# Rows gathered up to three units ahead and scaled in pieces, second products two columns behind the first

## The chip, the core and the metric

The kernel runs on one core of a Trainium2 chip. The core has five engines with an instruction queue each: TensorE (PE; its weight loads are listed as PEld), VectorE (DVE), ScalarE (ACT), GpSimd (POOL) and SyncE (SP), which here only issues transfers. Every queue is worked off in order. The metric is device time in microseconds (us), from first to last instruction of one launch. The kernel before took 943.5 us as the median of three timed runs (942.85 to 946.33). A change of 0.5% or less (4.7 us) counts as no change.

## The reference, cut to what matters

```python
def _attn_ref(q, k, v, tau):              # 8 batches, 8 heads, 576 tokens, 64 wide
    scores = (1 / sqrt(64)) * q @ k.T
    thresh = max(scores, -1) - tau
    scores = where(scores >= thresh, scores, -1e9)
    attn = exp(scores - max(scores)); attn /= sum(attn) + 1e-9
    return attn @ v

def _moe_ref(x, w_gate, w_output_gate, w1, w2):   # x: 4608 rows of 512; 8 experts, 1024 hidden
    logits = x @ w_gate; e_idx = argmax(logits); gate_w = softmax(logits)[e_idx]
    eom = sigmoid(x @ w_output_gate)
    for e in range(8):
        mask = e_idx == e
        h = maximum(x[mask] @ w1[e], 0); ye = h @ w2[e]
        out[mask] = gate_w[mask] * eom[mask, e] * ye
```

## The kernel before, in words

**Attention** (class Attention) runs first, in 144 steps, nine for a pair of units; a unit is one head of two batches. TensorE forms scores and their transposes, VectorE negates them and takes the minimum (L159) and masks the exponentials (L189), ScalarE takes the exponentials. Finished rows of 512 features, with gate weight and token number behind them, are routed and written by GpSimd's scatters to a table in device memory, `xs` (L547). Scatters of the first three batch pairs are called "A", those of the last pair "B". After B, eight "pad" scatters (L720) write empty rows behind each expert's last row.

**The experts** (class Experts) run as 13 units of one expert each, on rows that a gather on SP's queue brings from `xs` into a tile `xg`. Units 0, 1 and 2 are fixed groups of 366, 256 and 424 rows of experts 0 to 2, made of A rows alone. Units 3 to 12 have 420, 256, 512, 256, 504, 256, 396, 256, 256 and 496 rows; a table that VectorE fills step by step (`choose`) says which expert and rows they are. In what follows a unit of 256 rows is narrow, the others are wide. Each unit has eight **columns** of 128 hidden features. In column f TensorE does the first products of f (`first`, L1216, into `ph`), ScalarE applies the ReLU and rounds the result to 16 bits (`hr`, `hh`), VectorE forms the rest (`hl`, L955), and TensorE does the second products (`second`, L1238 to L1241; L1337 to L1340 in the "Turned" units 2, 3 and 9), which need `hh` and `hl`. Before, the second products of a column come right after the first products of the next.

Weights come in chunks of two columns. Each chunk is loaded, measured (largest value: VectorE's maximum L859 and ScalarE's `junk`, L867), scaled by a power of two and split into 16-bit high parts (ScalarE, L951) and low parts (VectorE, `w1l`, `w2l`, L957). The rows are treated alike: `even` finds the largest value of each row (`ax`, L911) and scales the tile (L916), four scalings for a wide unit; `prep` transposes it (TensorE, `px`, L1192 or L1314) and splits it (`xh`, `xl`). All this for unit i+1 is done during unit i: `even` at one go in column 3, `prep` in columns 5 and 6. Turned units are turned back by `flip` (L1354), which with `prep`, `top` and `spread` (two small products on the weights' scale) shares two tiles `px`.

The program order of TensorE, VectorE, ScalarE and GpSimd is the order in which the code is written (`manual_schedule`); `run` (L1064) writes it column by column. Transfers have their waits from the tiles and the rows of `xs` that they touch. Before, the scatters of A, B and pad are one group of the table to the framework, so a gather waits also for scatters whose rows it does not read.

Of the kernel before, what the change touches and what calls it, by code (L numbers as in the profile page):

```python
# [17 lines left out]
P = 128  # L18
# [412 lines left out]
class Router:  # L431
# [4 lines left out]
    def __init__(self, ctx, tc, ntok, E, DM, sizes, cut):  # L436
# [58 lines left out]
        self.gate, self.kind, self.pads = None, None, []  # L495
# [50 lines left out]
    def scatter(self, src, idx, group):  # L546
# [10 lines left out]
        return ins  # L557

    def route(self, bp, rows, LX):
# [82 lines left out]
        for b in range(n):  # L642
            yield "scatter"
            self.tok.append(("A" if split else "B", self.scatter(rows[:, b, :], dsti[:, b : b + 1], "tok")))
# [132 lines left out]
class Experts:  # L777
    RB, NW, YB = 4, 4, 4
    UNITS = (0, 6, 2, 7, 3, 8, 1, 5, 9, 4)
    TURN = (2,)  # L780
    LOOK, MEASURE = 3, 3

    def __init__(self, ctx, tc, rt, ident, w1, w2, out):
# [3 lines left out]
        self.raw = [self.pool("eraw", self.RB)]  # L787
        self.mp = self.pool("em", 1)
        self.junk = self.mp.tile([P, 1024], BF16, name="junk")
        self.early = self.mp.tile([P, 2 * rt.early, 4], F32, name="early")  # L790
        self.part = self.mp.tile([P, 1], F32, name="part")
# [3 lines left out]
        self.gp = self.pool("eg", 1)  # L795
# [9 lines left out]
    def open(self):  # L805
        self.px = lambda: [self.ps_x.tile([P, 512], F32, name="px") for _ in range(2)]
        self.hp = self.pool("eh", 2)
        self.ph = lambda: self.ps_h.tile([P, 512], F32, name="ph")
        self.hidden = lambda n: [self.hp.tile([P, 512], dt, name=x) for x, dt in (("hr", F32), ("hh", F16), ("hl", F16))]
        self.xp = self.pool("ex", 2)  # L810
        self.fp = self.pool("ef", 1)
        self.raw.append(self.pool("eraw1", self.RB))
        self.ahead = self.RB
        self.load_next()
        self.wp += [self.pool(f"ew{i}", 1) for i in range(1, self.NW)]
        for name, bufs in (("y", 4), ("h", 2), ("x", 2)):
            setattr(self, f"ps_{name}", self.pool(f"ps_{name}", bufs, space=PSUM))

# [36 lines left out]
    def measure(self, raw, mx, g, half=None):  # L855
        nc = self.nc
        flat = lambda r: r.rearrange("p c f -> p (c f)")
        if half is None:
            nc.vector.tensor_reduce(mx[:, 0, g : g + 1], flat(raw[0]), axis=AX.X, op=ALU.max, apply_absolute_value=True)  # L859
        else:  # L860
            part = flat(raw[0])[:, half * 512 : half * 512 + 512]
            to = mx[:, 0, g : g + 1] if half == 0 else self.part
            nc.vector.tensor_reduce(to, part, axis=AX.X, op=ALU.max, apply_absolute_value=True)
            if half == 0:
                nc.vector.tensor_tensor(to, to, self.part, op=ALU.max)
        if half != 1:
            nc.scalar.activation(self.junk, flat(raw[1]), AF.Abs, accum_out=mx[:, 1, g : g + 1])  # L867
# [40 lines left out]
    def even(self, xg):  # L908
        nc, n, DM = self.nc, xg.shape[1], self.rt.DM
        ax, up, down = (self.kp.tile([P, 4], F32, name=x)[:, 0:n] for x in ("ax", "xup", "xdown"))  # L910
        nc.vector.tensor_reduce(ax, xg[:, :, 0:DM], axis=AX.X, op=ALU.max, apply_absolute_value=True)  # L911
        nc.vector.tensor_scalar(ax, ax, UP, FLOOR, op0=ALU.mult, op1=ALU.max)
        self.powers(up, down, ax)
        for t in range(n):
            x = xg[:, t, 0:DM]
            nc.vector.tensor_scalar(x, x, up[:, t : t + 1], None, op0=ALU.mult)  # L916
        return down
# [51 lines left out]
    def begin(self):  # L969
# [7 lines left out]
        self.halves, self.ready, self.ahead, self.due = [], [], 0, None  # L977
        self.first_raws, self.column, self.fresh, self.mx, self.diag = [], 0, [], {}, None
        self.order = [(e, g) for e in (*range(1, rt.early), 0) for g in range(4)]
# [5 lines left out]
    def size(self, j, half=None):  # L985
        e, g = self.order[j]
        raw = self.first_raws[j]
        self.measure(raw, self.early[:, 2 * e : 2 * e + 2], g, half)
        if e == 0 and half != 1:
# [3 lines left out]
    def settled(self, i):  # L993
# [566 lines left out]
```

## Time and profile before

The profiled execution took 940.68 us with a span of 939.0 us; the median of the timed runs is 943.5 us.

| engine | busy us | share of the span | instructions |
|---|---|---|---|
| PE | 882.4 | 94% | 8367 |
| PEld | 539.5 | 57% | 8367 |
| DVE | 794.7 | 85% | 1940 |
| ACT | 708.8 | 75% | 1367 |
| POOL | 388.0 | 41% | 660 |

Busy time counts an instruction from its start to its end; matmuls overlap, so that a busy TensorE can still be waiting for less than the length of a matmul. Attention takes about the first half of the span; the first second products of unit 0 begin at 478.43 us. In the rows below, "[13.50 <-DVE hl L955]" means that the engine was idle for 13.50 us before this instruction, and that the instruction of line 955 which writes `hl` released it.

### The profile page before, as it was taken

Reading aid. Unit: us, or ns where it says so; the run is one execution under the profiler, and the core shown is the slowest. Engines: PE = TensorE matmul, PEld = TensorE weight load, DVE = VectorE, ACT = ScalarE, POOL = GpSimd, SP = SyncE. Lnnn points to the kernel's source line nnn. Section 1 sums busy time; section 2 is a strip of 40 time slices with the busy share of each in tenths; the row PEclk is TensorE's granted clock in tenths of the full one; section 3 lists DMA queues with packets and bytes.
Section 4 is the critical chain, followed back from the end, with each engine's and each line's share of the span. In section 5 each row is a group of like instructions: output and inputs, shape, how many; then the busy total and the mean of one; then the engine's idle time right before and its main releaser. Section 6 shows DMA issues by size and latency. Waiting matters only on the chain. (4 is left out here: it accounts for less than half of the span.)

```text
span 939.0 us, 22600 instructions
## 1 busy us (share of the span) xinstructions
PE 882.4 (94%) x8367; PEld 539.5 (57%) x8367; DVE 794.7 (85%) x1940; ACT 708.8 (75%) x1367; POOL 388.0 (41%) x660
## 2 busy tenths in 40 slices
PE   8999999999999999999899498798997997998996
PEld 4666666666666666666556254455444454565543
DVE  7999999999999999999978588979768667878841
ACT  6999999998999989899866275566656755777642
POOL 4455655758756687668547400202102102102101
PEclk9999999999999999999999799899998999999999
DMA  6499812153322444122178546345536525636001
GB/s 210 163 295 292 291 57 83 43 172 115 113 82 65 150 150 147 57 92 92 38 249 278 174 159 223 129 134 195 180 112 200 178 94 185 217 113 215 23 22 44
DMA packets 77009, 136.91 MB, mean 146 GB/s; under 512 B 6792, under 2 KB 37768, under 8 KB 76897
## 3 DMA queue, kind: packets, MB, share of 16 engines
q1 hardware_dynamic: 70353, 115.29, 38.6%
q0 software_dynamic: 6544, 20.16, 5.6%
q8 instruction: 66, 1.08, 0.5%
q14 instruction: 46, 0.38, 0.1%
HBM read 103.65 MB, written 32.74 MB: 145 GB/s over the span
## 5 line engine op out<-in xcount | busy, mean ns | idle before, releaser
L177 ACT ACTIVATE p<-s,mn 128x576 f32<-128x576 f32 x288 | 215.5, 798 | 26.1 <-DVE s L159 26.1
L189 DVE SCALAR_TENSOR_TENSOR p<-s,thr,p 128x576 f32<-128x576 f32 x288 | 226.2, 821 | 0.3 <-POOL thr L166 0.3
L159 DVE TENSOR_SCALAR_CACHE_REDUCE s<-ps 128x576 f32<-128x576 f32 x288 | 205.6, 749 | 14.1 <-PE ps L145 12.2
L145 PE MATMUL ps<-qk 64*128 64x288 f32 (+1 forms) x1280 | 184.5, 419 | 0.0
L939 POOL DMA_INDIRECT out_dram<-yo,kid x39 | 46.5, 1193 | 327.2 <-DVE yo L938 192.9
L166 POOL TENSOR_SCALAR thr<-mn,tau_sb 128x2 f32<-128x2 f32 x144 | 101.4, 704 | 135.6 <-DVE s L159 132.9
L1216 PE MATMUL ph<-xh,w1h 128*128 128x256 f16 (+7 forms) x412 | 132.6, 323 | 0.0
L1216 PE MATMUL ph<-xh,w1l 128*128 128x256 f16 (+7 forms) x412 | 131.7, 321 | 0.9 <-DVE w1l L957 0.7
L1216 PE MATMUL ph<-xl,w1h 128*128 128x256 f16 (+7 forms) x412 | 130.5, 321 | 0.0
L145 PEld LDWEIGHTS ps<-qk 64*128 64x128 f32 (+1 forms) x1280 | 110.6, 177 | 17.6 <-DVE s L159 3.0
L955 DVE TENSOR_TENSOR hl<-hr,hh 128x256 f16<-128x256 f32 (+7 forms) x103 | 54.4, 528 | 74.2 <-ACT hh L949 73.6
L1218 ACT ACTIVATE hr<-ph 128x256 f32<-128x256 f32 (+7 forms) x103 | 47.9, 465 | 88.8 <-PE ph L1216 85.2
L1216 PEld LDWEIGHTS <-w1h 128*128 128x128 f16 x832 | 80.5, 100 | 51.4 <-issue 2.5
L258 PE MATMUL pr<-PTb,vld 128*64 128x320 f32 (+1 forms) x640 | 107.2, 447 | 0.0
L244 PE MATMUL pt<-ident,p 64*128 64x64 f32 x2288 | 95.8, 223 | 1.7 <-ACT PTa L247 1.5
L1241 PE MATMUL py<-w2h,hl 128*128 128x512 f16 (+3 forms) x213 | 61.2, 386 | 27.0 <-DVE hl L955 26.9
L258 PE MATMUL pa<-PTa,vld 128*64 128x256 f32 (+1 forms) x640 | 84.6, 391 | 0.0
L244 PEld LDWEIGHTS pt<-ident,p 64*128 64x128 f32 x2288 | 82.8, 139 | 3.2 <-ACT PTa L247 2.7
L1238 PE MATMUL py<-w2h,hh 128*128 128x512 f16 (+3 forms) x213 | 81.4, 382 | 3.3 <-ACT hh L949 3.2
L1239 PE MATMUL py<-w2l,hh 128*128 128x512 f16 (+3 forms) x213 | 81.2, 381 | 0.0
L867 ACT ACTIVATE junk<-r 128x1024 bf16<-128x1024 f32 x52 | 55.4, 1066 | 24.5 <-DMA r<-in_moe_w_dram 22.5
L247 ACT COPY PTa<-pt 128x1024 f32<-128x1024 f32 x64 | 67.6, 1056 | 0.0
(240 smaller groups left out, 1721.7 us busy)
## 6 DMA issues: line engine op xcount, KB each, us to landing
r<-in_moe_w_dram SPq DMA_DIRECT2D x120, 512.0 KB, 4.2
qk<-in_qkv_dram SPq DMA_DIRECT2D x31, 608.0 KB, 3.9
xs<-zrow SPq DMA_DIRECT2D x44, 257.0 KB, 8.0
vld<-in_qkv_dram SPq DMA_DIRECT2D x32, 320.0 KB, 4.6
xg<-xs SPq DMA_DIRECT2D x4, 771.0 KB, 5.5
xg<-xs SPq DMA_DIRECT2D x6, 514.0 KB, 4.6
xg<-xs SPq DMA_DIRECT2D x3, 1028.0 KB, 8.4
xg<-xs SPq DMA_DIRECT2D x6, 128.5 KB, 6.2
```

Of the source, the lines that this page charges most:

```text
L145: nc.tensor.matmul(ps[a][rows, o : o + HS], q[pp, t * P : t * P + w], k[pp, k0 : k0 + HS], start=True, stop=True)
L159: nc.vector.tensor_scalar(s, ps[a][:, c0 : c0 + S], SC, None, op0=ALU.mult, op1=ALU.min, accum_out=mn[:, a : a + 1])
L166: self.router.gate = nc.gpsimd.tensor_scalar(thr, mn, self.tau, None, op0=ALU.add)
L177: self.nc.scalar.activation(e, ss[a], AF.Exp, bias=mn[:, a : a + 1], scale=-1.0)
L189: nc.vector.scalar_tensor_tensor(e, s, thr[:, a : a + 1], e, op0=ALU.is_le, op1=ALU.mult, accum_out=acc[:, a ^ (t > 1) : (a ^ (t > 1)) + 1])
L244: nc.tensor.transpose(pt[:, o : o + 64], p[hs[h], k0 : k0 + P], id_[hs[h], hs[h]])
L247: nc.scalar.copy(d, pt.rearrange("p (h b j) -> p b h j", h=2, j=64))
L258: one = lambda out, l, r, start, stop: nc.tensor.matmul(out, l, r, start=start, stop=stop, skip_group_check=True)
L1216: nc.tensor.matmul(ph, w[:, c, fs], x[:, c, 0:N], start=(i == 0), stop=(i == 11))
L1238: nc.tensor.matmul(Y, hh[:, ts], wh, start=(f == 0), stop=False)
L1239: nc.tensor.matmul(Y, hh[:, ts], wl, start=False, stop=False)
L1241: nc.tensor.matmul(Y, hl[:, ts], wh, start=False, stop=(f == 7))
```

## The change

- **Groups of scatters.** A, B and pad are groups of their own. Gathers of units 0 to 2 (`read_early`) depend on A alone, and B and pad scatters no longer depend on these gathers.
- **Row tiles.** Wide units share two tiles `xg` (one before, for all units), narrow units have a tile `xgn`. `gather_next` issues a gather as soon as the tile is free, for units from 3 on four columns after the pads are written.
- **Scaling in pieces.** `even` returns pieces (maxima of two row tiles, scalings of two). `level` issues one piece in each column of a wide unit, and in other columns only what the next unit needs by its `prep`. A unit's pieces follow its gather by at least `LOOK` = 4 columns.
- **Second products** come two columns behind the first (`back`), with three tiles `hh` and `hl` in place of two. `finish` and `flip` move by one column.
- **Weights.** Attention measures the chunks of experts 0 and 1 alone (`FIRST` = 2), each in one instruction; expert 2 is measured during unit 1. Splits are half a chunk further ahead; a chunk is measured four columns after its load (three before). `top` and `spread` of a unit fall into columns 0 and 1 of the one before (2 and 3 before), with exceptions for units 2 to 4 (`SCALE`).
- **Table and pads.** Picking steps (`aside`) come two to a column from unit 1 on; the last table (`finish` of the router) one step a column rather than six.

TensorE at the start of the experts, unit 0. `ph_8563` holds the first products of column 1, `py` second products, `h0h` the rounded hidden values of column 0. Before:

```order
L1216 MATMUL ph_8563<-xl_8383,w1h_8292 128x366
L1216 LDWEIGHTS w1l_8293
L1216 MATMUL ph_8563<-xh_8382,w1l_8293 128x366
L1238 LDWEIGHTS h0h_8462
L1238 MATMUL py_8582<-w2h_8294,h0h_8462 128x512
L1239 LDWEIGHTS h0h_8462
```

Now (`ph_8552` is column 1, `ph_8585` column 2, with the weights of the next chunk):

```order
L1260 MATMUL ph_8552<-xl_8369,w1h_8259 128x366
L1260 LDWEIGHTS w1l_8260
L1260 MATMUL ph_8552<-xh_8368,w1l_8260 128x366
L1260 LDWEIGHTS w1h_8524
L1260 MATMUL ph_8585<-xh_8368,w1h_8524 128x366
L1260 LDWEIGHTS w1h_8524
```

The second products of column 0 moved from behind column 1 to behind column 2.

VectorE in unit 1, columns 3 and 4: from one `hl` to the next, with unit 2's rows in `xg`. Before:

```order
L955 TENSOR_TENSOR hl<-hr,hh 128x256
L911 TENSOR_REDUCE ax<-xg 128x4
L912 TENSOR_SCALAR ax<-ax 128x4
L871 TENSOR_SCALAR xup<-ax 128x4
L872 TENSOR_SCALAR xdown<-ax 128x4
L916 TENSOR_SCALAR xg<-xg,xup 128x512 x4
L691 SCALAR_TENSOR_TENSOR key<-st 1x8
```

Now, columns 0 and 1 of the same unit (`r_8757` and `r_8819` are chunks of expert 2's weights, `mx` their largest values):

```order
L975 TENSOR_TENSOR hl<-hr,hh 128x256
L977 SCALAR_TENSOR_TENSOR w2l<-r_8532,upe,w2h 128x1024
L977 SCALAR_TENSOR_TENSOR w1l<-r_8573,upe,w1h 128x1024
L874 TENSOR_REDUCE mx<-r_8757 128x1
L701 SCALAR_TENSOR_TENSOR key<-st 1x8
L702 TENSOR_REDUCE mx<-key 1x1
L703 SCALAR_TENSOR_TENSOR cand<-key,mx,desc 1x8
L704 TENSOR_REDUCE cm<-cand 1x1
L706 TENSOR_SCALAR key<-key 1x8
L707 SCALAR_TENSOR_TENSOR cand<-cand,cm,key 1x8
L708 TENSOR_TENSOR pick<-st,cand 1x16
L709 TENSOR_REDUCE got<-pick 1x2
```

Unit 2's scaling left unit 1 (its pieces stand in unit 0), and measures of weights and a second picking step came in.

SP between attention and experts. `r_` tiles are weights; the 3x514 rows with 64x514 behind them are unit 2's. Before, with unit 2's gather after 18 weight transfers:

```order
L1158 DMA xg<-xs 128x3x514
L831 DMA r_8897<-in_moe_w_dram 128x4x256
L1158 DMA xg<-xs 128x2x514
L831 DMA r_8898<-in_moe_w_dram 128x2x512
...
L831 DMA r_9267<-in_moe_w_dram 128x2x512
L1369 DMA xg<-xs 128x3x514
L1369 DMA xg<-xs 64x514 x2
```

Now:

```order
L1205 DMA xg<-xs 128x3x514
L1205 DMA xgn<-xs 128x2x514
L1413 DMA xg<-xs 128x3x514
L1413 DMA xg<-xs 64x514 x2
L848 DMA r_8684<-in_moe_w_dram 128x4x256
L848 DMA r_8685<-in_moe_w_dram 128x2x512
```

The gathers of units 1 and 2 moved ahead of the weights of unit 1.

```diff
@@ class Router
-        if group == "pad":
-            self.tc.declare_no_dep(ins.ins, group="tok", reason="rows of their own")
+        others = {"A": (), "B": ("A",), "pad": ("A", "B")}[group]
+        for other in others + (("read",) if self.read else ()):
+            self.tc.declare_no_dep(ins.ins, group=other, reason="rows of their own")
         self.nodep(ins, group)
         return ins
+
+    def read_early(self, ins):
+        self.after(ins, [x for g, x in self.tok if g == "A"])
+        for group in ("B", "pad"):
+            self.tc.declare_no_dep(ins.ins, group=group, reason="rows of their own")
+        self.tc.add_to_no_dep_group("read", ins.ins)
+        self.read = True
@@ class Experts
+    FIRST = 2
+    LOOK = 4
+    SCALE = {2: (2, 4, 5), 3: (0, 1, 2), 4: (0, 1, 4)}
...
+        two = [(t, min(t + 2, n)) for t in range(0, n, 2)]
+        return down, [lambda f=f, ab=ab: f(*ab) for f in (most, scale) for ab in two]
...
+    def gather_next(self, i, f):
+        passed = i + (f > 6)
+        for line, room in self.lines:
+            while self.at[room] < len(line):
+                k = self.at[room]
+                if k >= room and line[k - room] > passed:
+                    break
+                n = line[k]
+                if n >= rt.early and not (self.known(n) and self.padded is not None and self.column > self.padded + 3):
+                    break
+                self.at[room] += 1
+                self.unit(n).gather()
+                self.since[n] = self.column
+
+    def level(self, i, k):
+        for n in sorted(self.since):
+            if self.column - self.since[n] >= self.LOOK or n == i + 1 and k >= -4:
+                del self.since[n]
+                self.pieces += [(n, x) for x in self.unit(n).even()]
+        self.pieces.sort(key=lambda x: x[0])
+        due = sum(n == i + 1 for n, _ in self.pieces)
+        count = max(int(self.unit(i).N > 2 * P), due + 1 + k if due else 0)
+        for _ in range(min(count, len(self.pieces))):
+            self.pieces.pop(0)[1]()
@@ run
-                if not (final and f == 7):
-                    if prev:
-                        prev[0].second(prev[1])
-                        if prev[1] == 7:
-                            prev[0].finish()
-                    prev = (b, f)
-                self.look(i, f, final)
...
-                if not final and k == -2:
-                    self.unit(i + 1).even()
...
-                for _ in range(6 if rt.last else 3 if i or f else 0):
+                self.scale(i, f)
+                back.append((b, f))
+                if len(back) > 2:
+                    p, pf = back.pop(0)
+                    p.second(pf)
+                    if pf == 7:
+                        p.finish()
...
+                self.split_until(2 * self.used + 4 + f % 2 - (i == 0))
+                self.look(i, f)
+                self.level(i, k)
+                for _ in range(1 if self.padded else 6 if rt.last else 3 if i or f else 0):
...
+                self.gather_next(i, f)
+                self.ahead = min(sum(self.RINGS), max(4, self.column + 2))
```

## Rows read from the trace of the kernel before

**Rows 1.** Attention, two passes of nine steps: length, busy us (instructions), clock, DMA share, GB/s
```profile
61.68:90.63 28.95, 28.71 (x368) 19.12 (x366) 28.42 (x79) 27.56 (x60) 16.81 (x27) 1.00 1.04 298
90.63:118.58 27.95, 27.95 (x368) 18.30 (x366) 27.42 (x76) 26.51 (x58) 16.79 (x27) 1.00 0.87 282
```

**Rows 2.** Tile `early`, VectorE: duration ns min/median/max, first and last start us
```profile
L859 DVE TENSOR_REDUCE early<-r x6: 1152/1156/1158, 40.0 to 354.8; 128x1 f32<-128x1024 f32 x6
L863 DVE TENSOR_REDUCE early<-r x6: 673/674/676, 53.2 to 397.5; 128x1 f32<-128x512 f32 x6
```

**Rows 3.** Timeline of PE, end of attention: start, us, instruction [idle before]
```profile
466.37 0.67 PE L1192 MATMUL ps<-ident,xg 64*128 64x64 f32 x4 [0.62 <-DVE xg L916]
467.52 0.47 PE L1192 MATMUL ps<-ident,xg 64*128 64x64 f32 x8 [0.48 <-DVE xg L916]
```

**Rows 4.** Stretches of units 0 to 3; last, VectorE's to column 24
```profile
476.42:505.08 28.66, 27.92 (x170) 15.59 (x169) 24.94 (x66) 18.96 (x30) 18.26 (x24) 1.00 0.91 311
505.08:544.41 39.33, 25.71 (x176) 16.29 (x175) 24.80 (x67) 17.16 (x34) 18.96 (x16) 0.83 0.55 174
544.41:584.51 40.10, 37.06 (x217) 19.86 (x215) 36.92 (x101) 24.99 (x42) 2.29 (x3) 0.96 0.60 204
584.51:629.54 45.03, 38.94 (x230) 21.93 (x227) 37.50 (x84) 28.33 (x47) 5.03 (x5) 0.92 0.39 133
476.42:588.60 112.18, 94.78 (x583) 53.95 (x582) 90.23 (x244) 64.31 (x112) 39.51 (x42) 0.92 0.66 219
```

**Rows 5.** Waits of PE from 476.42 us on: total us, times, longest
```profile
PE py L1241 <- DVE hl L955: 26.9, 5, 13.5
PE px L1354 <- DVE most L888: 8.4, 3, 6.1
...
PE px L1314 <- DVE down L872: 3.0, 1, 3.0
```

**Rows 6.** Waits of PE from 629.54 us on (units 4 to 12)
```profile
PE py L1241 <- DVE hl L955: 13.4, 4, 5.1
PE py L1238 <- ACT hh L949: 3.2, 3, 1.2
PE px L1354 <- DVE most L888: 2.3, 2, 1.1
```

**Rows 7.** Waits of SP's queue
```profile
SPq L1369 <- DMA xs<-zrow,padi: 11.5, 1, 11.5
```

**Rows 8.** Timeline of VectorE, unit 1
```profile
527.82 2.29 DVE L911 TENSOR_REDUCE ax<-xg 128x4 f32<-128x2048 f32 x1 [10.92 <-DMA xg<-xs]
```

**Rows 9.** VectorE's groups from 476.42 us on: busy us, mean ns, idle before
```profile
L957 DVE SCALAR_TENSOR_TENSOR w1l<-r,up,w1h 128x1024 f16<-128x1024 f32 x40 | 51.0, 1275 | 0.0
L859 DVE TENSOR_REDUCE mx<-r 128x1 f32<-128x1024 f32 x40 | 48.3, 1209 | 0.0
L911 DVE TENSOR_REDUCE ax<-xg 128x2 f32<-128x1024 f32 x6 | 7.3, 1210 | 0.0
L693 DVE SCALAR_TENSOR_TENSOR cand<-key,mx,desc 1x8 f32<-1x8 f32 x10 | 2.2, 222 | 0.4
```

**Rows 10.** Timelines of VectorE and PE, unit 4
```profile
644.87 2.27 DVE L911 TENSOR_REDUCE ax<-xg 128x4 f32<-128x2048 f32 x1
647.66 1.68 DVE L916 TENSOR_SCALAR xg<-xg,xup 128x512 f32<-128x512 f32 x4
650.92 0.61 PE L1241 MATMUL py<-w2h,hl 128*128 128x512 f16 x2 [1.75 <-DVE hl L955]
```

**Rows 11.** Stretches of unit 4 (narrow) and unit 5 (wide)
```profile
629.54:658.16 28.62, 25.72 (x201) 17.53 (x200) 24.33 (x40) 19.38 (x36) 5.07 (x5) 1.00 0.59 195
658.16:699.49 41.33, 41.33 (x206) 18.71 (x205) 28.30 (x42) 27.48 (x41) 2.53 (x3) 1.00 0.45 148
```

**Rows 12.** Stretches behind the two waits of 5 us, units 6 and 8
```profile
722.60:727.60 5.00, 5.00 (x32) 3.04 (x33) 5.00 (x7) 2.33 (x4) 0.00 (x0) 0.50 0.60 202
796.40:799.50 3.10, 3.05 (x22) 1.80 (x23) 3.10 (x5) 1.04 (x5) 0.00 (x0) 0.50 0.55 169
```

More of the change, by code (lines that the diff above doesn't have):

```diff
@@ L494, in __init__ @@
         self.xrows, self.queue, self.pending, self.placed, self.tables = {}, [], None, None, []
-        self.gate, self.kind, self.pads = None, None, []
+        self.gate, self.kind, self.pads, self.read = None, None, [], False
     def aside(self, n):
@@ L908, in even, with most, scale, rows_tile @@
     def even(self, xg):
-        nc, n, DM = self.nc, xg.shape[1], self.rt.DM
+        V, n, DM = self.nc.vector, xg.shape[1], self.rt.DM
         ax, up, down = (self.kp.tile([P, 4], F32, name=x)[:, 0:n] for x in ("ax", "xup", "xdown"))
[L911 to L917, printed above, removed]
+        def most(a, b):
+            V.tensor_reduce(ax[:, a:b], xg[:, a:b, 0:DM], axis=AX.X, op=ALU.max, apply_absolute_value=True)
+            if b == n:
+                V.tensor_scalar(ax, ax, UP, FLOOR, op0=ALU.mult, op1=ALU.max)
+                self.powers(up, down, ax)
+        def scale(a, b):
+            for t in range(a, b):
+                V.tensor_scalar(xg[:, t, 0:DM], xg[:, t, 0:DM], up[:, t : t + 1], None, op0=ALU.mult)
+        two = [(t, min(t + 2, n)) for t in range(0, n, 2)]
+        return down, [lambda f=f, ab=ab: f(*ab) for f in (most, scale) for ab in two]
+    def rows_tile(self, nt):
+        if nt == 2:
+            return self.gn.tile([P, 2, self.rt.W], F32, name="xgn")
+        self.wide += 1
+        return self.gp[(self.wide - 1) % len(self.gp)].tile([P, 4, self.rt.W], F32, name="xg")
     def keys(self, xg, back=None, down=None):
@@ L977, in begin @@
         self.halves, self.ready, self.ahead, self.due = [], [], 0, None
+        tiles = [-(-(rt.base[n] if n < rt.early else rt.SLOTS[self.UNITS[n - rt.early]]) // P) for n in range(len(make))]
+        self.lines = [([n for n, t in enumerate(tiles) if t > 2], 2), ([n for n, t in enumerate(tiles) if t == 2], 1)]
+        self.at, self.since, self.wide, self.pieces = {2: 1, 1: 1}, {1: -self.LOOK}, 0, []
         self.first_raws, self.column, self.fresh, self.mx, self.diag = [], 0, [], {}, None
-        self.order = [(e, g) for e in (*range(1, rt.early), 0) for g in range(4)]
+        self.order = [(e, g) for e in (*range(1, self.FIRST), 0) for g in range(4)]
     def glance(self, j):
@@ L1030, in load_next @@
                 return
-            k = i % 2
-            raw = self.load(self.unit(i).e, g, k=k)
-            if i >= self.rt.early:
+            a, b = self.RINGS
+            raw = self.load(self.unit(i).e, g, k=int(self.nload % (a + b) >= a))
+            if i >= self.FIRST:
                 self.fresh.append((self.nload, raw, self.column))
@@ L1072, in run @@
             for f in range(8):
-                ahead = f // 2 in b.w and f == 0
-                if f % 2 == 0 and not ahead:
+                done = f == 0 and 0 in b.w
+                if f % 2 == 0 and not done:
                     b.w[f // 2] = self.take()
-                if not ahead:
+                if not done:
                     b.first(f)
@@ L1154, in gather @@
         ex, rt, e = self.ex, self.ex.rt, self.e
[L1155 removed]
+        self.xg = ex.rows_tile(self.nt)
         early = e < rt.early
         r0 = rt.A + rt.at[e] if early else e * rt.CAP
+        assert early
         ins = self.nc.sync.dma_start(
@@ L1160, in gather @@
         )
-        rt.after(ins, [x for g, x in rt.tok if g == "A" or not early])
-        if not early:
-            rt.after(ins, rt.pads)
-        else:
-            assert sum(g == "A" for g, _ in rt.tok) == 9 * (rt.cut + 1)
+        rt.read_early(ins)
     def even(self):
-        self.down = self.ex.even(self.xg[:, 0 : self.nt])
+        self.down, pieces = self.ex.even(self.xg[:, 0 : self.nt])
+        return pieces
     def key(self):
@@ L1369, in load @@
         ins = self.nc.sync.dma_start(dst, src if n < P else src.rearrange("(t p) w -> p t w", p=P))
-        rt.after(ins, [x for g, x in rt.tok if g == "A"])
+        rt.read_early(ins)
 class Flex:
@@ L1473, in build @@
                 hooks[end - 4] = lambda: ex.unit(0).gather()
+                hooks[end - 2] = lambda: ex.unit(1).gather()
                 hooks[end - 1] = lambda: ws.extend(ex.first_chunk())
@@ L1480, in prep, with even @@
                     ex.unit(0).prep(k, outs)
+                def even():
+                    for piece in ex.unit(0).even():
+                        piece()
                 def begin():
-                    prep(0)
                     ws[0]()
```

136 lines of the change are left out of this document (60 added, 76 removed).

## The prediction, made before the changed kernel was run

> **What bounds the kernel now.** First the page: TensorE is busy for 94% of the span and no other engine for more than 85%. That average hides stages with different limits, so I read the stretches next, stage by stage.
>
> In attention TensorE shows almost no idle time, 28.71 of 28.95 us and 27.95 of 27.95 [rows 1]. Still two passes with the same 368 matmuls differ by 1.00 us. In the longer one VectorE has three more instructions: beside a whole measure of 1.16 us it takes one in halves, 2 x 0.67 us, and their maximum [rows 2], and its busy time rises by 1.00 us, from 27.42 to 28.42. TensorE follows VectorE there, and its matmuls merely look longer.
>
> The Trainium skill ("Perfetto Trace Analysis", section "Identifying the Most-Contended Engine") says that matmul busy time is a poor measure of how near TensorE is to its limit, since matmuls are pipelined. The trace agrees: 99 to 100% busy at two lengths. Whoever took the busy share as the bound would put attention's part of this change at zero.
>
> Between attention and experts TensorE waits 0.62 and 0.48 us for the scaled rows of unit 0 [rows 3]. In units 0 to 3 VectorE is nearly as loaded as TensorE: in unit 2 36.92 of 40.10 us, TensorE 37.06 [rows 4]. Here TensorE's waits are long: 13.5 us once and 6.1 us once, besides 3.0 us [rows 5]. The 13.5 us have a chain: unit 2's gather waits 11.5 us on SP's queue for the pad scatters [rows 7], whose rows it does not read; VectorE, in program order, stands 10.92 us at this gather's `ax` [rows 8]; the `hl` behind it comes late. From unit 4 on, a narrow unit has 25.72 us of TensorE's work in 28.62 us; a wide one 41.33 in 41.33, with VectorE busy for only 28.30 of them [rows 11]. The waits there sum to 13.4 + 3.2 + 2.3 = 18.9 us [rows 6]. Behind them the clock falls: two stretches of 5.00 and 3.10 us show 0.50, the 1.2 GHz level [rows 12], after waits of some 5 us.
>
> **The change, part by part.** The sum is made against the profiled execution (940.68 us, span 939.0), which lies 2.8 us under the median of the timed runs.
>
> *Attention: -4.5 us.* Six chunks measured in halves leave it, two whole measures come into passes that had none. By the two passes [rows 1] a chunk in halves costs a pass 1.00 us, the only price I see for one. The whole measure I take at 1.16 us of VectorE's time, of which by the same relation at most 0.75 is new in the path: -6 x 1.00 + 2 x 0.75 = -4.5. Ends: 0, if the two passes differ for another reason, and -6.7, if half of the whole measures' cost is hidden.
>
> *Turn to the experts: -1.0 us.* The waits of 0.62 and 0.48 us [rows 3] go, as the transposes are issued a step later, behind the scaling. Ends 0 and -1.1.
>
> *Units 0 to 3: -4.5 us.* The three waits that lie in them sum to 13.5 + 3.0 + 6.1 = 22.6 us: of the kinds in [rows 5], those before 629.54 us, thus without the rows of [rows 6]. The gather of unit 2 now precedes the weights in SP's queue and depends on A alone, so the 11.5 us on the pads are off and so is VectorE's stand of 10.92 us. But what is late next? From the first second products to the end of unit 2's columns on VectorE are 112.18 us, of which VectorE is busy for 90.23 [rows 4]. Into this stretch the change brings:
> - six measures of weights, four of expert 2 (formerly in attention) and two of later chunks: 6 x 1.21 = 7.3 us [rows 9];
> - the scaling of unit 4, formerly in unit 3: `ax` of two tiles 1.21 [rows 9], two scalings of 1.68 / 4 = 0.42 each and 0.5 for the powers between 647.14 and 647.66 [rows 10], 2.6 us; and the two maxima of unit 5, 2 x 1.21 = 2.4 us;
> - one low part more by the half chunk of lead, 1.3 us [rows 9];
> - seven picking steps of three or four instructions, 26 x 0.222 = 5.8 us [rows 9], an upper value.
>
> Together 19.4 us, and 90.2 + 19.4 = 109.6. The last 2.6 us of the 112.18 are small gaps, in front of `hl` and `xl`, that stay since VectorE waits there for ScalarE. So VectorE becomes the bound, and up to there nothing is gained: the wait moves from one place of 13.5 us to several, where TensorE needs an `xl` or `w1l` that VectorE has not reached. In the start the lag of two columns also asks for a chunk's weights a column's second products sooner, about half of 27.92 / 8 = 3.5 us [rows 4], 1.7 us that VectorE's load already contains. In unit 3 the wait of 6.1 us goes: before it stand six steps of the last table in a column, now one. I subtract 1.5 us for low clock behind the new waits; the price is half of a stretch like the second in [rows 12]. -6.1 + 1.5 = -4.6, say -4.5. Ends: +2 if the lag's 1.7 us come on top and the 6.1 us merely move, and -25 if the backlog on VectorE never reaches TensorE: 22.6 us of waits, 4.8 of low clock in the proportion found below (4.05 behind 18.9), less 2 for the start.
>
> *Units 4 to 12: -20.9 us.* Before, in column 3, a wide unit's `ax` of 2.27 us and four scalings of 1.68 us stand on VectorE in front of the `hl` for which TensorE waits 1.75 us; the longest such wait is 5.1 us [rows 6, 10]. Now the pieces stand mostly in columns of wide units, where VectorE has 41.33 - 28.30 = 13 us spare, and second products wait for an `hl` one column older. A narrow unit's column takes 25.72 / 8 = 3.2 us of TensorE [rows 11], so a piece of 1.21 us fits in the slack. The 18.9 us go; so does half of the two half-clock stretches, (5.00 + 3.10) / 2 = 4.05 us [rows 12]. I leave 2 us for waits on `hh` and for the tiles `px`, which `top`, `spread`, `flip` and `prep` still share. -18.9 - 4.05 + 2 = -20.9. Ends: -23 with no such remainder, -11.5 if half of waits and low clock return.
>
> *The tail* (the last unit's output) has no edit in it: 0.
>
> Sum: -4.5 - 1.0 - 4.5 - 20.9 = -30.9; 940.7 - 30.9 = 909.8 profiled, and with the 2.8 us 912.6: **913 us** timed.
>
> **Rivals.**
> *A, VectorE's backlog stays hidden.* The order gives TensorE one column more slack, and small gaps of VectorE close. Then units 0 to 3 give -25 + 4 for a remainder like that of the late units, in place of -4.5: 913 - 16.5 = 896 us. For it: VectorE's sum of 109.6 us is still under 112.2. Against: TensorE has only 94.78 us of work in that stretch [rows 4], far less than VectorE.
>
> *B, half of the late waits return.* In a narrow unit in front of a wide one, all four pieces must come in its columns 1 to 4, one each, beside measures and splits, with VectorE busy for 24.33 of 28.62 us [rows 11]; and the wait for a `px` tile passes from one product to the next. Late units give -11.5 + 2 and not -20.9: 913 + 11 = 924 us. Against: the total of VectorE's work there does not rise.
>
> *C, the change does not do what it says.* Unit 2's gather stays late for another reason, such as a scatter of A or the tile's former rows: VectorE stands again for some 11.5 us [rows 7], with its load moved behind it: 924 us. Against: at the pads' wait the releaser is named, and A's scatters were done when units 0 and 1 gathered.
>
> *D, slower.* With VectorE as the bound in units 1 to 3, TensorE works in short groups between many short waits and is granted 1.2 GHz through much of them. Its busy time there is 25.71 + 37.06 + 38.94 = 101.7 us [rows 4]. All of it at half clock adds 101.7 us, of which the idle time of the same windows (124.5 - 101.7 = 22.8 us) swallows a part. This decides from the point at which the loss, less 22.8, equals the other parts' gain of 26.4 us: at 49 us, about half of the work. At three quarters the early units give 76.3 - 22.8 = +53.5, and the time is 940.7 - 26.4 + 53.5 + 2.8 = 971 us. Against: unit 4 keeps clock 1.00 through waits like the 1.75 us [rows 10, 11], and low clock shows behind waits of some 5 us [rows 12].
>
> The Trainium skill speaks for D ("TensorE: Matmul & The Clock Gate", section "A second HAM failure mode: psum-queue depth-cycling"): short idles between groups of matmuls can make the clock swing, and throughput falls. In this trace unit 4 with its waits of 1 to 2 us at clock 1.00 does not show it; it is no more than a reason for D's chance.
>
> **How the numbers follow.** My forecast 0.60 (its own range 904 to 924: attention from 0 to -6.7, late units from -23 to -15, units 0 to 3 within 5 us), A 0.12, B 0.16, C 0.05, D 0.07. The range reaches to A and to B, C and a little beyond: 894 to 932; the ends of the terms, added up, would give 887 and 935. A measurement can tell 0.5%, 4.7 us, from no change. Faster: the forecast, A and most of B and C, 0.90; the same, where B and C come together or D just decides, 0.04; slower, the rest of D, 0.06.
>
> **What would show it.** Right: SP's wait of 11.5 us on the pads and the wait of 13.5 us for `hl` are gone; attention's passes that had halves are 1.0 us shorter; VectorE is busy for over 90% of units 1 and 2, with waits of TensorE of 3 to 7 us, in sum over 10 us, for `xl` or weights at first columns; from unit 4 on no wait of over 1.2 us and clock 1.00. Wrong: waits in units 0 to 3 under 5 us (A), waits from unit 4 on over 8 us (B), a long idle of VectorE for unit 2's `xg` (C), or a clock of 0.5 to 0.7 over whole units (D).

## The result, and the profile after

The changed kernel took 917.4 us as the median of four timed runs, against 944.2 us for the kernel before on the same chip: a ratio of 0.971 (95% interval 0.969 to 0.973), 26.8 us less. The forecast was 913 us. The profiled execution of the changed kernel took 915.95 us with a span of 914.2 us; against 940.68 us that is 24.7 us less, and it divides as follows. Each piece ends where TensorE works on the same matmuls of both kernels.

| stage | before us | after us | difference | forecast |
|---|---|---|---|---|
| up to unit 0's first products | 473.3 | 467.3 | -6.0 | -5.5 |
| units 0 to 3 | 156.2 | 156.2 | 0.0 | -4.5 |
| units 4 to 12 and the tail | 309.5 | 290.7 | -18.8 | -20.9 |

The rows of these stretches, first of the kernel before (units 0 to 3 from their first products, then the rest), then of the changed kernel (length, then busy us and instructions of PE, PEld, DVE, ACT and POOL, clock, DMA share, GB/s):

```profile
473.31:629.54 156.23, 132.74 (x816) 75.89 (x815) 124.69 (x317) 90.87 (x154) 44.54 (x47) 0.92 0.58 194
629.54:939.00 309.46, 283.10 (x1737) 159.25 (x1735) 214.45 (x337) 191.10 (x316) 39.37 (x38) 0.98 0.41 137
```
```profile
467.30:623.53 156.23, 132.54 (x806) 74.22 (x805) 139.22 (x352) 95.48 (x163) 41.11 (x47) 0.95 0.64 205
623.53:914.20 290.67, 281.12 (x1749) 160.41 (x1747) 205.50 (x321) 189.94 (x315) 44.59 (x38) 0.99 0.42 137
```

The first row of each pair tells the surprise: units 0 to 3 are not a hundredth shorter, while VectorE does 14.5 us more in them. The second rows hold the gain: the work of TensorE is nearly the same, the time around it shrank.

Two attention passes, as in [rows 1]. Both now have the shorter one's length and its number of VectorE instructions:

```profile
60.53:88.50 27.97, 27.97 (x368) 18.30 (x366) 27.43 (x76) 26.51 (x58) 16.80 (x26) 1.00 1.04 314
88.50:116.47 27.97, 27.97 (x368) 18.31 (x366) 27.44 (x76) 26.52 (x58) 16.80 (x26) 1.00 0.63 211
```

Waits of TensorE in units 0 to 3, which answer to [rows 5] (total us, times, longest):

```profile
PE px L891 <- DVE red L886: 7.6, 2, 4.5
PE px L891 <- DVE red L885: 6.0, 1, 6.0
PE px L673 <- DVE ohb L588: 3.1, 1, 3.1
PE ph L1260 <- DVE xl L975: 2.4, 2, 1.2
PE ph L1260 <- DVE w1l L977: 1.9, 1, 1.9
PE py L1285 <- DVE hl L975: 0.8, 1, 0.8
PE ph L1260 <- ACT w1h L971: 0.7, 1, 0.7
PE py L1282 <- ACT yo L956: 0.6, 1, 0.6
PE px L1358 <- DVE down L880: 0.5, 1, 0.5
```

The waits of 13.5, 6.1 and 3.0 us are gone, as is SP's wait on the pads, and others of 23.6 us in sum stand in their place. The largest, 13.6 us, are at L891, the transposition of a unit's largest weights `red`. VectorE's order around the 6.0 us shows why (start, us, instruction):

```profile
517.85 1.27 DVE L977 SCALAR_TENSOR_TENSOR w2l<-r,upe,w2h 128x1024 f16<-128x1024 f32 x1
519.04 1.21 DVE L874 TENSOR_REDUCE mx<-r 128x1 f32<-128x1024 f32 x1
...
521.55 1.27 DVE L977 SCALAR_TENSOR_TENSOR w1l<-r,upe,w1h 128x1024 f16<-128x1024 f32 x1
522.75 1.20 DVE L874 TENSOR_REDUCE mx<-r 128x1 f32<-128x1024 f32 x1
524.05 0.16 DVE L885 TENSOR_REDUCE red<-mx 128x2 f32<-128x8 f32 x1
```
```profile
524.57 0.37 PE L891 MATMUL px<-ident,red 128*2 128x128 f32 x1 [5.98 <-DVE red L885]
```

VectorE is busy for 5.7 of these 6.0 us; the fourth measure of expert 2, which attention took before, comes right in front of `red`. From unit 4 on one wait of 2.0 us is left, in front of the transposes of unit 11's rows, against the 18.9 us of [rows 6].

### The profile page after: what moved, and what is told of

It reads as the page before. It is cut to its first block, busy times and chain, and to the rows that moved or that the text cites. A ratio compares the mean times of both kernels' runs of the same rounds, so it can differ in the third digit from the quotient of the medians.

```text
span 914.2 us, 22624 instructions
## 1 busy us (share of the span) xinstructions
PE 875.4 (96%) x8369; PEld 534.8 (59%) x8369; DVE 795.8 (87%) x1941; ACT 708.8 (78%) x1367; POOL 389.9 (43%) x660
## 5 line engine op out<-in xcount | busy, mean ns | idle before, releaser
L959 POOL DMA_INDIRECT out_dram<-yo,kid x39 | 49.7, 1274 | 330.9 <-DVE yo L958 234.7
L145 PE MATMUL ps<-qk 64*128 64x288 f32 (+1 forms) x1280 | 181.1, 418 | 0.0
L166 POOL TENSOR_SCALAR thr<-mn,tau_sb 128x2 f32<-128x2 f32 x144 | 103.3, 718 | 129.7 <-DVE s L159 125.8
L1260 PE MATMUL ph<-xh,w1h 128*128 128x256 f16 (+7 forms) x412 | 131.6, 320 | 0.7 <-ACT w1h L971 0.7
L145 PEld LDWEIGHTS ps<-qk 64*128 64x128 f32 (+1 forms) x1280 | 107.2, 177 | 17.5 <-DVE s L159 2.5
L324 POOL TENSOR_TENSOR rows<-xl,rinv 128x256 f32<-128x256 f32 x64 | 62.1, 971 | 11.3 <-ACT xl L369 11.0
L247 ACT COPY PTb<-pt 128x1024 f32<-128x1024 f32 x63 | 65.1, 1034 | 1.2 <-PE ps L145 1.1
```

The source lines that it names most:

```text
L145: nc.tensor.matmul(ps[a][rows, o : o + HS], q[pp, t * P : t * P + w], k[pp, k0 : k0 + HS], start=True, stop=True)
L166: self.router.gate = nc.gpsimd.tensor_scalar(thr, mn, self.tau, None, op0=ALU.add)
L247: nc.scalar.copy(d, pt.rearrange("p (h b j) -> p b h j", h=2, j=64))
L324: nc.gpsimd.tensor_tensor(o, xl[:, a, 0:4, 0:D], ra[:, a, 0:4, None].broadcast_to([P, 4, D]), op=ALU.mult)
L1260: nc.tensor.matmul(ph, w[:, c, fs], x[:, c, 0:N], start=(i == 0), stop=(i == 11))
```

## The experiments

All times are medians of four or five runs, each beside runs of the kernel before on the same chip (944.1 to 945.1 us). "The changed kernel" is 917.4 us. Lengths of stages are those of one profiled execution each.

**1. One column of lag.**

```diff
-                if len(back) > 2:
+                if len(back) > (2 if final and f == 7 else 1):
```

> The changed kernel (917.4 us) with the second products one column behind the first again, as before. Theory 1 (VectorE is the bound from the last column of unit 0 to the first of unit 3; the lag of two columns costs some 4 us at the start of the experts and pays from unit 4 on): the start of column 3 of unit 0 comes 3 to 4 us sooner, but from unit 4 on waits for hl of 1 to 2 us return in the columns with pieces of scaling, 3 to 8 us in sum: 915 to 922 us. Theory 2 (the lag itself holds TensorE back in units 0 to 3, VectorE's load does not): the waits for the scale products in units 1 to 3 (16 us in sum) shrink by half or more: 905 to 911 us.

917.2 us, ratio to before 0.971 (0.970 to 0.972): no difference to the changed kernel. No wait for `hl` came back: from unit 4 on the trace lists one wait alone.

```profile
PE px L1236 <- issue: 2.0, 1, 2.0
```

Both theories had a part wrong. Units 0 to 3 are no shorter with one column (157.5 us): TensorE's waits at the scale products fall from 13.6 to 8.4 us there, but waits of 8.0 us for `hl` come back. And beside the pieces the second column of lag pays nothing later: units 4 to 12 and the tail take 289.2 us with one column and 290.7 us with two.

**2. One column of lag in unit 0 alone.**

```diff
+                if len(back) > (2 if i else 1):
```

> The changed kernel with the second products one column behind in unit 0 alone, two columns from unit 1 on. Theory 1 (VectorE bound up to unit 3): TensorE comes 3 to 4 us sooner to column 3 of unit 0 and gives nearly all of it back in the first long wait in unit 1, since VectorE's own row of work is as long as before: 915.5 to 917.5 us. Theory 2 (the loss of the start is a loss of the end): 912 to 914 us.

917.4 us, ratio 0.971 (0.969 to 0.972). From first products to column 3 of unit 0 take 16.6 us, as in the changed kernel, against 12.0 us in the kernel before. But with one column of lag TensorE has two columns of second products behind it there, and one with two columns; a column of them takes 1.9 us. So the lag had cost the start some 2 us, about half of what theory 1 said, and units 0 to 3 are no shorter without it (157.6 us). The waits there are for `hh` (1.6 us) and the one-hot tile (2.4 us), and fewer for weights (0.7 us).

**3. Without four measures.**

```diff
+        if n // 4 == 2:
+            self.nc.vector.memset(self.mx[2][:, 0, n % 4 : n % 4 + 1], 0.2)
...
```

> The changed kernel without VectorE's four measures of expert 2's first weights; a constant of 0.2 stands in for the four largest values, so this work is left out. Theory 1 (VectorE bound): four instructions of 1.20 us less on VectorE in unit 1, the waits for the scale products fall by as much: 911 to 913.5 us. Theory 2 (VectorE's load hidden): 916.5 to 918 us.

914.2 us, ratio 0.968 (0.967 to 0.970): 3.2 us less for 4.8 us of VectorE's work. In the profiled execution 1.4 us of it lie in units 0 to 3 (154.8 us) and 1.8 us in the later ones, which the edit does not touch: there a stretch of low clock is missing, though the wait in front of it is the same (last section). Theory 1 had the direction; its size, 4 us and more, is not borne out, and run 12 tells more of VectorE's load.

**4. Unit 2's gather late again.** The gather is held back to column 0 of unit 1 and not taken out of the groups of B and pad.

```diff
+                if n == 2 and (i, f) < (1, 0):
+                    break
...
-        rt.read_early(ins)
+        rt.after(ins, [x for g, x in rt.tok if g == "A"])
```

> The changed kernel with unit 2's gather issued in column 0 of unit 1 behind the weight transfers and after the pad scatters, as before; its scaling follows in unit 1, a part in each column. Theory 1: the rows land near 528 us, VectorE stands 8 to 10 us at the first maximum and has the same work behind it: 924 to 928 us. Theory 2 (the early gather is worth nothing since VectorE's load is hidden anyway): 917 to 920 us.

931.0 us, ratio 0.986 (0.984 to 0.988): 13.6 us more, beyond both theories. The gather goes out at 522.9 us, 3.0 us later than in the kernel before (519.9), and VectorE, which comes to these rows at 516.6 us (516.9 before), stands longer than the 10.92 us of [rows 8]; behind it comes more work than before:

```profile
531.43 1.22 DVE L921 TENSOR_REDUCE ax<-xg 128x2 f32<-128x1024 f32 x1 [14.81 <-DMA xg<-xs]
```
```profile
536.92 0.37 PE L891 MATMUL px<-ident,red 128*2 128x128 f32 x1 [19.86 <-DVE red L886]
```

**5. The groups alone, in the kernel before.** Groups of scatters and `read_early`, no other part of the change.

```diff
-        rt.after(ins, [x for g, x in rt.tok if g == "A"])
+        rt.read_early(ins)
```

> The kernel before (944.9 us) with the groups of scatters alone: gathers of units 0 to 2 wait for A's scatters only. The gather of unit 2 then lands before VectorE needs it; the wait of 13.5 us on TensorE and the stand of 10.9 us on VectorE go. My theory (in the kernel before VectorE has 90 us of work in the 112 us of that stretch, so the wait's end is a gain until other waits bind): 933 to 937 us. Rival (the pads' wait is replaced by the next transfer or scatter that is late): 941 to 945 us.

932.8 us, ratio 0.988 (0.987 to 0.990), 11.3 us less, at the edge of my range. VectorE has the load of before and units 0 to 3 take 144.1 us:

```profile
477.12:621.18 144.06, 131.63 (x817) 75.66 (x815) 124.42 (x317) 90.89 (x154) 45.04 (x47) 0.95 0.62 210
621.18:930.20 309.02, 282.99 (x1737) 159.22 (x1735) 214.58 (x337) 191.12 (x316) 39.16 (x38) 0.98 0.41 138
```

So the early gather is worth 12.2 us in these units, and the rest of the change takes all of it back there. The second row shows that it does nothing from unit 4 on. (The first products come 3.8 us later than in the profile of before, which is why the times differ by less; 1.4 us of that are passes of attention that the groups change, see "Attention" below, and 0.9 us the first pass, which varies by as much among runs with the same attention.)

**6. Expert 2 measured in attention.** Twelve whole measures, in passes 1 to 10, 12 and 15.

```diff
-    FIRST = 2
+    FIRST = 3
...
+                size = (1, 2, 3, 4, 5, 6, 7, 8, 9, 10, 12, 15)
```

> The changed kernel with expert 2's four chunks measured in attention again, each whole, in passes 5 to 8, and expert 0's in passes 9, 10, 12 and 15. The run without these four measures gained 3.2 us in the experts. Theory 1 (attention pays at most 0.75 us for a whole measure in a pass): 914.5 to 917.5 us. Theory 2 (attention pays the full 1.2 us for each, 4.8 us): 918 to 920 us.

915.3 us (912.1 to 917.5), ratio 0.969 (0.967 to 0.971). In its profiled execution units 0 to 3 take 148.6 us, 7.6 less, and attention ends 9.1 us later. 5.8 us of these are passes 7 and 8, in which VectorE stood twice, 2.5 us for GpSimd's `thr` and 2.4 us for TensorE; that execution was the slowest of the five. Passes 5, 9 and 10, which have no measure in the changed kernel, became 0.8, 0.8 and 0.1 us longer. Theory 1 fits. By the medians this version is 2.1 us faster, at the edge of what they can tell: that attention measures one expert fewer was no gain in time. The edit takes more than four measures out of units 0 to 3: unit 2's scale products, with the wait of 6.0 us at L891, and ScalarE's four sums leave them too.

**7. The whole scaling in one column, with two columns of lag, and 8. with one.**

```diff
-            if self.column - self.since[n] >= self.LOOK or n == i + 1 and k >= -4:
+            if n == i + 1 and k == -2:
...
-        for _ in range(min(count, len(self.pieces))):
+        for _ in range(len(self.pieces)):
```

> The changed kernel (917.4 us; two columns between first and second products; gathers early) with a unit's whole scaling in one column again, three columns ahead of its transposes, as before. The run with one column of lag showed no late wait, so lag is not needed where the scaling is in pieces. Theory A (pieces and lag can stand in for each other: either covers the 4 us of scaling): no wait of over 1 us from unit 4 on, 915 to 920 us. Theory B (the pieces alone remove the late waits): waits of 2 to 5 us return at units 4, 6 and 8, 927 to 936 us.

> As the run before it, and the second products one column behind the first: both edits undone, early gathers kept. Theory A (either covers): now the late waits return, 10 to 20 us: 927 to 938 us. Theory B: the same waits as with two columns, 927 to 936 us. Theory C (the early gathers alone removed the late waits): 915 to 920 us.

918.0 us, ratio 0.973 (0.971 to 0.974), and 921.3 us, ratio 0.977 (0.975 to 0.979). The stretches from unit 4 on, of the two:

```profile
620.48:916.50 296.02, 282.45 (x1749) 160.69 (x1747) 213.31 (x338) 189.72 (x315) 41.30 (x38) 0.99 0.41 134
```
```profile
623.01:919.40 296.39, 280.35 (x1737) 158.54 (x1735) 212.87 (x338) 189.24 (x315) 40.89 (x38) 0.99 0.40 134
```

With two columns the first theory's time came out, but the stage is 5.3 us longer than in the changed kernel (290.7 us), which units 0 to 3 made good (152.7 us against 156.2): scaling that the changed kernel does ahead stands from unit 4 on again, so VectorE works 7.6 us less in units 0 to 3 (131.6 us) and 7.8 us more after them. With one column, and neither cover left, units 0 to 3 take 155.3 us, and the stage behind them is still 13 us shorter than before: the larger part of the late waits stays away without pieces and lag. By the times, either cover alone does what both do (917.2 and 918.0 us, with both 917.4), and without either 3 to 4 us are lost (921.3), the pattern of theory A at a third of its size or less. Theory C was nearest, and late rows were the next suspect.

**9. Also with late gathers.**

```diff
+                if n > rt.early and not (n <= i + 1 or n == i + 2 and f == 7):
+                    break
```

> The changed kernel with one column of lag and the whole scaling in one column (921.3 us, 8.5 us of waits for TensorE from unit 4 on), and from unit 4 on each gather issued only in the last column of the unit two before its own, as in the kernel before, where VectorE stood 1.8 us twice for rows that had not landed. Theory A (the late waits of the kernel before were late rows as much as scaling): waits of TensorE from unit 4 on rise to 13 us and more, 925 to 931 us. Theory B (the time of the gathers does not matter there): 920 to 922.5 us.

923.3 us, ratio 0.977 (0.976 to 0.978); from unit 4 on 296.6 us, with waits of 8.6 us (8.5 in run 8). Theory B's time, but the edit had not made the rows late: they were issued 12.1 us sooner than in the kernel before, 4.6 us of which are that the stage begins sooner. SP's queue, first the kernel before, then this run (start, us, transfers; unit 7's rows are the last `xg` of each):

```profile
669.73 37.69 SPq L831 DMA_DIRECT2D r<-in_moe_w_dram  x8
707.67 0.37 SPq L1282 DMA_DIRECT2D xg<-xs  x1
```
```profile
660.00 35.32 SPq L848 DMA_DIRECT2D r<-in_moe_w_dram  x8
695.53 0.37 SPq L1328 DMA_DIRECT2D xg<-xs  x1
```

In both the gather stands behind eight weight transfers, which wait for VectorE's low parts to free their tiles. These low parts are half a chunk further ahead now. In the kernel before VectorE then stood for these rows, ahead of the scaling behind which TensorE waited 5.0 us:

```profile
716.53 2.29 DVE L911 TENSOR_REDUCE ax<-xg 128x4 f32<-128x2048 f32 x1 [1.79 <-DMA xg<-xs]
```

**10. Also the splits less ahead and last in a column, from unit 4 on.**

```diff
-                self.split_until(2 * self.used + 4 + f % 2 - (i == 0))
+                if i <= rt.early:
+                    self.split_until(2 * self.used + 4 + f % 2 - (i == 0))
...
+                if i > rt.early:
+                    self.split_until(2 * self.used + 3 + f % 2)
```

> The run with late gathers (923.3 us; whole scaling in one column, one column of lag, 8.6 us of waits for TensorE from unit 4 on), and from unit 4 on also the split of weights last in each column and half a chunk less ahead, as in the kernel before. In the kernel before the gather of unit 7 stood in SP's queue behind weight transfers that wait for VectorE's low parts and was issued at 707.7 us, 9.0 us before VectorE could begin on its rows; in the run with late gathers it was issued at 695.5 us. Theory A (the lead of the splits, through SP's queue and the order on VectorE, removed the larger part of the late waits): waits from unit 4 on rise to 14 us and more, 929 to 936 us. Theory B (the tiles for the rows or the new columns of the scale products removed it): 922 to 926 us.

934.0 us, ratio 0.988 (0.985 to 0.990), 10.8 us more than run 9. The stage is as long as before (308.6 us), the waits are back, and VectorE stands for rows, as in the kernel before:

```profile
PE py L1290 <- DVE hl L975: 15.8, 5, 5.7
```
```profile
701.47 0.37 SPq L1331 DMA_DIRECT2D xg<-xs  x1
```
```profile
711.01 1.22 DVE L921 TENSOR_REDUCE ax<-xg 128x2 f32<-128x1024 f32 x1 [3.05 <-DMA xg<-xs]
```

Theory A: the lead of the splits and their place in the column were worth 12.0 us of the late units (308.6 to 296.6), in a kernel that has the gathers as late as before, the whole scaling in one column and one column of lag. How much of it is the lead and how much the place was not tried apart; nor was whether the early gathers or the pieces would have removed these waits by themselves, with the splits as before.

**11. The router's steps first in unit 0's columns.**

```diff
+                if not i:
+                    side()
                 self.split_until(2 * self.used + 4 + f % 2 - (i == 0))
```

> The changed kernel with the router's and the table's steps ahead of splits, measures and scaling in each column of unit 0, as in the kernel before. TensorE's wait of 3.1 us for the one-hot tile in column 2 of unit 0 goes; column 3 of unit 0 starts 2 to 3 us sooner. Theory 1 (VectorE is the bound from unit 1 on and gives it back): 915.5 to 918 us. Theory 2 (a loss at the start is a loss at the end): 913 to 915 us.

915.6 us, ratio 0.968 (0.967 to 0.970). The wait for the one-hot tile fell from 3.1 to 0.7 us, column 3 came 2.0 us sooner after the first products, and units 0 to 3 took 154.4 us. The medians lie 1.8 us apart, just at the edge of what they can tell; the time lies at the lower edge of theory 1.

**12. ScalarE measures the first weights of units 2 and 3.**

```diff
+        if n // 4 in (2, 3):
+            for h in range(2):
+                flat = raw[h].rearrange("p c f -> p (c f)")
+                self.nc.scalar.activation(self.junk, flat, AF.Abs, accum_out=self.mx[n // 4][:, h, n % 4 : n % 4 + 1])
+            return
```

> The changed kernel with the first weights of units 2 and 3 measured by ScalarE (the sum of absolute values, as it does for the second weights) in place of VectorE: eight instructions of 1.2 us less on VectorE in units 1 and 2, eight of about 1.1 us more on ScalarE, which is busy there for 21 of 34 and 26 of 42 us. Theory 1 (VectorE bound up to unit 3; four such measures left out gained 3.2 us): 909 to 913 us. Rival (ScalarE, which forms hr and hh and the high parts, comes late in its place): 915 to 920 us.

912.9 us, ratio 0.967 (0.965 to 0.968): the fastest version, 4.5 us under the changed kernel. Units 0 to 3 took 151.8 us; VectorE worked 9.0 us less in them and ScalarE 8.9 more:

```profile
467.42:619.25 151.83, 132.43 (x807) 74.20 (x806) 130.20 (x344) 104.39 (x179) 41.78 (x47) 0.96 0.64 211
```

The wait at L891 fell from 13.6 to 5.5 us, and TensorE now waits for ScalarE too (`hr` 1.7 us, `yo` 2.7). Theory 1.

## Why the prediction was right, and where not

**Attention, -4.5: the size right, in part by luck.** The same product at the end of the last pass starts at 457.16 us and started at 461.66, 4.5 us sooner. Run 5, which has the halves and the groups of scatters, splits them in two. Against it the six passes that had halves are 0.9 to 1.0 us shorter (from a pass's first score product to that of the next), 5.8 us in sum where 6.0 were forecast. The two new whole measures cost 0.1 us in pass 6 and nothing in pass 15, not 0.75 each. That these 5.7 us became 4.5 is mostly the groups' doing, which the forecast put at nothing: with the groups alone passes 7, 11 and 14 are 0.15, 0.8 and 1.2 us longer than before and passes 8 and 12 are 0.2 and 0.5 us shorter, 1.4 us in sum. Passes 11 and 14, the kernel before and the changed one:

```profile
316.11:344.08 27.97, 27.97 (x369) 18.30 (x365) 27.28 (x79) 25.40 (x54) 19.05 (x30) 1.00 0.36 116
403.23:431.20 27.97, 27.97 (x370) 18.33 (x366) 27.75 (x85) 25.81 (x56) 20.52 (x35) 1.00 0.27 94
```
```profile
312.19:340.89 28.70, 28.18 (x368) 18.40 (x366) 27.49 (x80) 25.65 (x55) 19.53 (x31) 1.00 0.27 84
397.53:426.95 29.42, 28.72 (x370) 18.93 (x366) 28.19 (x85) 25.68 (x55) 21.40 (x37) 1.00 0.30 99
```

In run 5 these two passes take 28.7 and 29.2 us, and in all versions of the changed kernel 28.7 to 28.8 and 29.4 to 29.5. By which wait the groups cost attention this was not tried.

**Turn, -1.0: right**, -1.5 measured; the waits of [rows 3] are gone.

**Units 0 to 3, -4.5: the step that failed**, with 0.0 measured, inside the ends of +2 and -25. Right in it: the pads' wait goes, the 6.1 us go, VectorE's work rises about as summed, and no time is won up to unit 3. What failed is the term for VectorE's gaps. In the stretch of 112.18 us [rows 4] VectorE was busy for 90.2 us and idle for 22.0, 10.9 of them at unit 2's rows. The forecast let the busy time rise to 109.6 us and the idle time shrink to 2.6. The same stretch, in the changed kernel and with the groups alone (run 5):

```profile
470.41:588.32 117.91, 97.35 (x586) 53.88 (x584) 107.00 (x289) 73.14 (x127) 36.48 (x42) 0.94 0.70 222
480.23:580.37 100.14, 93.80 (x583) 53.76 (x582) 89.97 (x244) 64.33 (x112) 40.02 (x42) 0.97 0.72 245
```

VectorE is busy for 107.0 us, 2.6 less than forecast, but 10.9 us of gaps stay, as 10.2 do with the groups alone. So the stretch became 5.7 us longer, and the 5.7 us won behind it, to the end of unit 3 (40.9 to 35.2 us, where the 6.1 us stood), only make that good.

That VectorE's load takes away the 12.2 us of the groups is borne out in part. It has 14.5 us more to do in units 0 to 3, and work taken off it gives time back, but not all of it: runs 3, 7, 8 and 12 take 4.7 to 8.9 us off VectorE in that stretch, and it becomes 1.7 to 3.0 us shorter. Run 6, which also takes unit 2's scale products out of TensorE's order, wins 7.9 us for 6.0. So the place of the scale products may count as much as the load; putting them back alone was not tried, and the cause stays open to that extent.

At the start, column 3 comes 16.6 us after the first products, not 12.0, and with a column of second products less done. Some 2 us of this are the lag's (runs 1 and 2), near the 1.7 of the forecast. The other 4.5 us, with one column of lag, are mostly waits of 1.6 us for `hh` and 2.4 us for the one-hot tile: splits and scaling now stand in front of the router's steps (run 11 took 2.0 us away). The new wait stands at the scale products, where I had named `xl` and weights. The order shows, on TensorE, the product on `red` ahead of the next second products, and on VectorE the four measures ahead of `red`; the two read together would have named the place.

**Units 4 to 12, -20.9: the size nearly right, the reason only in part.** -18.8 measured. I put the waits down to the scaling in one go and to the short slack, and gave the pieces and the lag the credit. In the trace's stages with one scaling column and one of lag 296.4 us are left of 309.5; pieces then take 7.2 us more (289.2 with one column of lag), or 5.3 us with two, of which units 0 to 3 give 2.2 and 3.5 us back; the lag takes 0.4 us off or puts 1.5 on, the size of what one profile can tell. Of the 13 us that are left without both, 12.0 go with the lead and place of the splits, and with rows and weights that come sooner through SP's queue (runs 9 and 10); whether other parts of the change would have won them alone is open. I read the 1.75 us of unit 4 [rows 10], where the rows were in time, for a type of all; at the waits of 5 us VectorE had stood 1.8 us for rows before it began to scale.

**The rivals.** A is out: VectorE's backlog reached TensorE. B is out for the time, 2.0 us of late waits being left. C is out: VectorE no longer stands for unit 2's rows; run 4 shows what a late gather costs, 13.6 us where I gave it 11, with rows 3.0 us later than before. D is out: in units 0 to 3 the mean clock rose from 0.92 to 0.95, with more and shorter waits than before. What I held against D was too strong, though: the clock fell behind two waits of 2.0 us too, and in the kernel before already behind the one of 3.0 us (below). As to the rule of the Trainium skill on short idles ("TensorE: Matmul & The Clock Gate", section "A second HAM failure mode: psum-queue depth-cycling"), the traces show falls behind single waits of about 2 us and more, not behind each of them, and none that swings through a whole unit.

**The signs.** The pads' wait, the 13.5 us and the half measures are gone, VectorE is over 90% busy in units 1 and 2 (32.4 of 34.5 us and 40.0 of 41.9) and the late units have one wait of over 1.2 us; waits in units 0 to 3 were 23.6 us where "over 10" was named. Two ends in the prediction do not follow from their conditions: half of the whole measures' cost hidden gives -5.25 and not -6.7 for attention, and the terms of the forecast's own range reach to 928 and not 924. The measured time lies within either.

## What to carry to other kernels

When a wait ends, add up the busy time of the engine that stood there together with all that the change puts on it, and its gaps too, since they need not close: here VectorE got 14.5 us of new work and the 12.2 us of gain went. Giving some of that work to a neighbour with time to spare (ScalarE's sums, run 12) won 4.5 us. In a queue that carries both weights and rows, what frees the weights' tiles decides when the rows come; look at what stands in front of a late transfer before blaming what comes after it. Two covers for one wait (pieces and lag) have to be tried singly: here either alone did what both do.

## What was not expected of the hardware

A 128x1024 maximum on VectorE (1.16 us) cost a pass of attention 0.0 to 0.8 us where it stood whole (the two passes of run 6 with long stands of VectorE left out), and 0.9 to 1.0 us where it stood in halves (0.67 us each and the maximum of the two). That VectorE was busy for 98% of those passes did not tell the two apart.

In the kernel before a wait of 1.75 us left the clock at 1.00, and low clock showed behind each wait of 3.0 us and more. Behind the one of 3.0 us:

```profile
577.30:581.10 3.80, 3.80 (x23) 1.92 (x24) 2.83 (x14) 3.17 (x7) 0.00 (x0) 0.58 0.25 94
```

In the changed kernel it fell to 0.50, the 1.2 GHz level, behind a wait of 1.95 us (with one of 0.73 us shortly before) and behind one of 1.97 us:

```profile
475.70:478.20 2.50, 2.46 (x9) 1.24 (x10) 1.07 (x1) 2.26 (x3) 0.41 (x2) 0.50 1.03 373
...
833.90:836.40 2.50, 2.50 (x15) 1.76 (x14) 1.82 (x3) 2.12 (x3) 0.00 (x0) 0.50 0.02 7
```

The length of the wait does not settle it. The wait of 3.1 us for the one-hot tile left the clock of the changed kernel at 1.00, and in run 3 so did the same wait of 1.97 us in front of unit 11's rows:

```profile
483.80:486.30 2.50, 2.50 (x17) 1.52 (x18) 2.27 (x6) 0.35 (x2) 1.98 (x2) 1.00 1.08 367
```
```profile
832.90:835.40 2.50, 2.50 (x19) 1.66 (x17) 2.01 (x3) 2.47 (x5) 0.00 (x0) 1.00 0.03 7
```

So a wait of 2 us can cost more than itself, by an estimate from the 2.5 us at 0.50 over a microsecond, or nothing more.
